# A hand-written order of a linear-attention and feed-forward block, laid out anew behind unchanged loads

## The chip, the cores and the metric

One core of a Trainium2 chip runs the whole program. The metric is the device time of one execution in microseconds (us); every time below is in us unless marked ns. Five engines work beside each other, each through its own queue in order: TensorE (PE; PEld is its weight load), VectorE (DVE), ScalarE (ACT), GpSimd (POOL) and SyncE (SP), which here only issues DMAs.

## The reference

Two blocks in a row on x of 2048 x 512, in bfloat16. Block A is linear attention with 32 heads of 16, block B a feed-forward layer with ReLU of width 1792. Both normalise their input and add their result to it.

```python
qkv = layernorm(x) @ wqkv                    # q, k, v: 32 heads of 16
phi = lambda t: where(t > 0, t + 1, exp(t)) + 1e-6
pq, pk = phi(q), phi(k)
kv = einsum("bhsd,bhse->bhde", pk, v)        # over all 2048 tokens
z = einsum("bhsd->bhd", pk)
o = einsum(pq, kv) / (einsum(pq, z) + 1e-6)
h = x + o @ wo
out = h + maximum(layernorm(h) @ w1, 0) @ w2
```

## The kernel before

The 2048 tokens are 16 tiles of 128 (index t, 0 to 15), four to a chunk (index c, 0 to 3). The program is a list of words in the string ORDER (lines 18 to 53). A word such as K.5.1 calls op_K(5, 1), which issues a few instructions of one engine. The last numbers of a TensorE word name one of the eight banks of the matmul memory, bk; of an ACT or DVE word, how many tiles or banks it takes at once. Each engine runs its own words in the order of the list. Where a word needs what another engine or a DMA makes, or a buffer or bank that another engine still reads, it waits, and everything behind it on its engine waits too. So the list fixes five queues and the use of the banks, and nothing else of the time.

Phase 1, per tile: S and A (lines 237, 238) are the statistics of the norm and their aggregate on VectorE, R (line 257, two activations at 243 and 244) the reciprocal deviation on ScalarE, N (line 260) the normalised tile on VectorE, written to h_nat. It is transposed into lnT either on TensorE and copied out by ScalarE (T, E: lines 284, 290; tiles 0 to 3) or by a transposing DMA (X, line 302; tiles 4 to 15). K (line 306) is the product with the weights of k, four matmuls of 128x512. F is its exponential and U its ReLU on ScalarE (lines 328, 331), M clips the exponential and D adds the two on VectorE (lines 335, 338): the feature map pk. W (line 343) does ReLU and addition in one. G (line 360) adds pk's product with the normalised tile into banks 4 to 7 over all 16 tiles. za and zf (lines 367, 371) add pk up for z on VectorE, z (line 377) finishes it on TensorE, zc and zh copy and mask it (lines 386, 389). Q with qF, qU, qM, qD, qW is the same as K, F, U, M, D, W for the queries, by chunk and by column block.

Phase 2: gA (line 394) copies the sum of G out on ScalarE, kv (line 400) multiplies it by the weights of v, kx masks it, m (line 413) multiplies by wo, mA copies that out. Per chunk, dn (line 454) is the denominator on TensorE, dnl and dnx (lines 464, 470) its logarithm and the exponential of its negative on ScalarE, written to wk_sb, two tiles a word. It is transposed into rd by DMA (dt, line 489) or on TensorE with a copy (rt, rv, re). rd holds one chunk. dm (line 493) multiplies the queries by it, h (line 501) is the product with m, and hD (line 510) adds x.

Phase 3: s, a, n (lines 239, 240, 268) are the second norm; its deviation r (line 258) is used at the end. n is transposed by DMA (x, line 303) or on TensorE (t, e). p (line 517) is the product with w1, pA or pD its ReLU on ScalarE or VectorE (lines 526, 531), f (line 537) the product with w2, fourteen matmuls in two halves, fo (line 547) the scaling and addition on VectorE, fd (line 554) the store. Tile 15 is done in a half and two quarters, a quarter last.

Loads are DMAs of SyncE: lx (x), lk, lq, lv, lo, l1, l2 (weights). Matmuls on zeros (warm, warmf, lines 213 and 218) run until the first tile comes.

```python
for word in ORDER.split():
    name, *idx = word.split(".")
    ops[name](*map(int, idx))
```

Of the kernel before, what the change touches and what calls it, by code (L numbers as in the profile page):

```python
# [38 lines left out]
p.0.10.3 hD.8 dt.15 s.8 a.6 pD.0.6.2 a.4 pA.0.10.2 n.6 f.1.1.0.7 hD.9 n.7 f.1.1.7.7 s.9 dm.3.0.2 dm.3.2.2 h.11.7  # L39
a.5 n.5 h.12.2 h.15.6 h.14.4 fo.1 h.10.5 hD.11 f.0.7.0.7 hD.12 x.6 a.8 h.13.1 a.9 f.3.3.0.7 f.3.3.7.7 x.7 hD.15  # L40
n.4 hD.14 f.0.7.7.7 x.4 f.2.0.0.7 hD.13 fo.3 x.5 p.1.0.6 s.12 s.11 n.8 hD.10 fo.0 p.1.1.7 a.11 fd.0 p.1.5.3 s.10
pD.1.0.2 f.2.0.7.7 a.12 n.12 n.9 s.14 p.1.4.2 n.11 p.1.8.4 fo.2 p.1.3.1 r.4.4 a.10 a.14 p.1.13.7 p.1.2.0
pD.1.4.2 n.10 x.10 x.11 s.13 p.1.7.2 p.1.9.5 p.1.12.6 a.13 pD.1.2.2 s.15 a.15 pD.1.8.2 n.14 pD.1.12.2 p.1.6.1
n.15 x.9 x.8 pA.1.6.2 f.7.0.0.7 p.1.10.4 fd.1 p.1.11.5 pD.1.10.2 fd.3 f.5.2.0.7 p.2.9.7 p.2.11.5 f.7.0.7.7
f.5.2.7.7 fo.7 p.2.8.6 p.2.10.4 p.2.5.1 pD.2.10.2 p.2.4.0 r.8.4 pA.2.8.2 f.4.4.0.7 fo.5 p.2.2.5 fd.2 pA.2.4.2
p.2.3.6 n.13 f.4.4.7.7 p.2.1.3 x.12 p.2.0.2 f.6.0.0.7 x.14 pA.2.2.2 fo.4 x.13 x.15 p.3.3.7 p.3.7.5 p.3.2.6
r.12.4 p.3.9.4 f.6.0.7.7 pA.2.0.2 p.3.11.1 p.3.8.3 p.3.4.2 fd.4 fd.5 fo.6 pA.3.8.2 pD.3.2.2 p.3.10.0 p.3.5.3
p.3.6.4 pA.3.10.2 fd.7 pA.3.6.2 p.2.6.6 pD.3.4.2 p.2.7.7 pD.2.6.2 p.3.13.5 p.3.1.1 fd.6 p.2.12.6 p.3.0.0
# [543 lines left out]
```

## Time and profile before

| what | us |
|---|---|
| median of 3 runs | 170.09 |
| lowest, highest run | 170.05, 170.57 |
| span of the profiled execution, first to last instruction | 168.8 |
| TensorE busy in it | 163.1 |
| VectorE busy | 104.4 |
| ScalarE busy | 65.1 |

The page gives no other time for the profiled execution than its span; the runs' median lies 1.3 above it. A line of the views has a start and a length in us, then engine, source line, operation, what is written and read, shapes and the count of instructions; brackets give idle time of the engine just before and what ended it. The ends of matmuls are modelled: a group of them is through for the next one earlier than its row ends.

### The profile page before, as it was taken

The page shows a single profiled execution, that of the slowest core. Times are in us where ns is not written, and L with a number is a line of the kernel's source. Part 1 is how long each engine was busy: PE and PEld are TensorE (multiplying, and loading weights), DVE is VectorE, ACT ScalarE, POOL GpSimd, SP SyncE. Part 2 cuts the span into 40 slices and gives each one's busy share as a digit, 9 for nine tenths or more (in the row PEclk, how much of TensorE's full clock was granted, in tenths as well). Part 3 has the DMA queues.
Part 4 walks back from the last instruction along what each step waited for, and adds up shares of the span by engine and source line. Part 5 has one row for each costly group of instructions (what it writes and reads, how often), then busy time and mean ns, then how long its engine had stood idle before and what let it go on. Part 6 is the DMA issues. An engine that isn't in the chain of part 4 may idle for free.

```text
span 168.8 us, 2286 instructions
## 1 busy us (share of the span) xinstructions
PE 163.1 (97%) x855; PEld 78.0 (46%) x871; DVE 104.4 (62%) x205; ACT 65.1 (39%) x97; POOL 4.8 (3%) x21
## 2 busy tenths in 40 slices
...
DMA packets 30491, 15.49 MB, mean 92 GB/s; under 512 B 23184, under 2 KB 29328, under 8 KB 30480
## 3 DMA queue, kind: packets, MB, share of 16 engines
...
q8 instruction: 7, 0.11, 0.3%
...
HBM read 7.86 MB, written 2.10 MB: 59 GB/s over the span
## 4 chain that ended last, share of the span: by engine, by line
PE 85%; DVE 7%; DMA 4%; issue 1%; SPq 0%
PE bk L541 29%; PE bk L521 28%; PE bk L505 8%; PE bk L318 8%; PE bk L362 6%; PE bk L310 4%; DVE st L237 3%; DMA x_nat<-in_A_x_dram 2%; DMA lnT<-h_nat 2%; DVE h_nat L262 2%; PE bk L459 1%; DVE eb L335 1%; PE bk L403 1%; PE bk L415 1%; SPq L201 0%
## 5 line engine op out<-in xcount | busy, mean ns | idle before, releaser
L541 PE MATMUL bk<-w_sb,at 128*128 128x512 bf16 (+2 forms) x247 | 50.1, 355 | 0.3
L521 PE MATMUL bk<-lnT,w_sb 128*128 128x512 bf16 x219 | 50.0, 379 | 0.3
L527 ACT ACTIVATE at<-bk 128x1024 bf16<-128x1024 f32 x14 | 14.2, 1023 | 57.4 <-PE bk L521 57.4
L541 PEld LDWEIGHTS <-at 128*128 128x128 bf16 x252 | 23.6, 98 | 25.4 <-ACT at L527 0.3
L549 DVE SCALAR_TENSOR_TENSOR gT<-bk,rstd,h_nat 128x512 bf16<-128x512 f32 (+2 forms) x18 | 12.2, 689 | 35.7 <-PE bk L541 35.6
L521 PEld LDWEIGHTS <-w_sb 128*128 128x128 bf16 x224 | 21.8, 98 | 25.8
L532 DVE TENSOR_SCALAR at<-bk 128x1024 bf16<-128x1024 f32 x14 | 17.1, 1218 | 12.8 <-PE bk L521 12.6
L328 ACT ACTIVATE eb<-bk 128x1024 bf16<-128x1024 f32 (+1 forms) x18 | 16.6, 928 | 6.6 <-PE bk L310 4.8
L310 PE MATMUL bk<-wk_sb,lnT 128*128 128x512 bf16 x63 | 15.3, 380 | 0.4 <-ACT lnT L291 0.3
L505 PE MATMUL bk<-m_sb,pqs 128*128 128x512 bf16 x63 | 15.4, 380 | 0.1
L318 PE MATMUL bk<-lnT,wq_sb 128*128 128x512 bf16 x61 | 15.1, 379 | 0.1
L362 PE MATMUL bk<-at,h_nat 128*128 128x512 bf16 x55 | 13.5, 379 | 0.1
L331 ACT ACTIVATE rb<-bk 128x1024 bf16<-128x1024 f32 (+1 forms) x14 | 12.5, 904 | 0.3 <-PE bk L310 0.3
L511 DVE TENSOR_TENSOR h_nat<-bk,x_nat 128x512 bf16<-128x512 f32 x16 | 10.5, 680 | 2.9 <-PE bk L505 2.9
L237 DVE BATCH_NORM_STATS2 st<-x_nat 128x6 f32<-128x512 bf16 x16 | 10.8, 680 | 2.4 <-DMA x_nat<-in_A_x_dram 2.4
L239 DVE BATCH_NORM_STATS2 st<-h_nat 128x6 f32<-128x512 bf16 x16 | 10.7, 683 | 0.1
L310 PEld LDWEIGHTS <-lnT 128*128 128x128 bf16 x64 | 6.0, 98 | 8.4 <-ACT lnT L291 1.0
L362 PEld LDWEIGHTS <-h_nat 128*128 128x128 bf16 x64 | 6.2, 98 | 7.4 <-issue 0.2
L505 PEld LDWEIGHTS <-pqs 128*128 128x128 bf16 x64 | 5.9, 98 | 7.9 <-DVE pqs L495 1.8
L318 PEld LDWEIGHTS <-wq_sb 128*128 128x128 bf16 x64 | 5.9, 98 | 6.4
L472 ACT ACTIVATE wk_sb<-ld 128x1024 bf16<-128x1024 f32 x8 | 8.1, 1050 | 0.1
L335 DVE TENSOR_SCALAR eb<-eb 128x1024 bf16<-128x1024 bf16 (+1 forms) x18 | 6.8, 383 | 0.9 <-ACT eb L328 0.9
...
## 6 DMA issues: line engine op xcount, KB each, us to landing
...
w_sb<-in_B_w_dram SPq DMA_DIRECT2D x2, 384.0 KB, 3.5
...
```

Source lines behind the costliest of these rows:

```text
L237: op_S = lambda t: nc.vector.bn_stats(out=st[:, t, :], in_=x_nat[:, t, :])
L310: nc.tensor.matmul(bk[:, b, :], lhsT=lnT[c][:, kd, j * P : (j + 1) * P], rhs=wk_sb[:, kd, :], start=(kd == 0), stop=(kd == KD - 1),)
L318: nc.tensor.matmul(bk[:, b, :], lhsT=wq_sb[:, kd, j * P : (j + 1) * P], rhs=lnT[c][:, kd, :], start=(kd == 0), stop=(kd == KD - 1),)
L328: nc.scalar.activation(out=buf(eb, kind, i, n), in_=bank(at_bank[kind, i], n), func=ACT.Exp)
L331: nc.scalar.activation(out=buf(rb, kind, i, n), in_=bank(at_bank[kind, i], n), func=ACT.Relu)
L362: nc.tensor.matmul(bk[:, KD + kd, :], lhsT=ln_nat[:, t, kd * P : (kd + 1) * P], rhs=pk(t)[:, 0, :], start=(t == 0), stop=(t == NT - 1),)
L505: nc.tensor.matmul(bk[:, b, :], lhsT=pqs[:, (c * KD + jb) % NQ, j * P : (j + 1) * P], rhs=m_sb[:, jb, :], start=(jb == 0), stop=(jb == KD ...
L521: nc.tensor.matmul(bk[:, b, cols], lhsT=w1_sb[:, kd, f * P : (f + 1) * P], rhs=lnT[c][:, kd, cols], start=(kd == 0), stop=(kd == KD - 1),)
L527: nc.scalar.activation(out=acts[c % 2][:, f : f + n, :], in_=bank(at_bank["p", c, f], n), func=ACT.Relu)
L532: nc.vector.tensor_scalar(out=acts[c % 2][:, f : f + n, :], in0=bank(at_bank["p", c, f], n), scalar1=0.0, scalar2=None, op0=ALU.max,)
L541: nc.tensor.matmul(bk[:, b, 0 : w * P], lhsT=acts[c % 2][:, f, j * P : (j + 1) * P], rhs=w2_sb[:, f, k * P : (k + w) * P], start=(f == 0), ...
L549: nc.vector.scalar_tensor_tensor(out=o_t[:, t % NO, cols], in0=bk[:, at_bank["f", t, k], 0 : w * P], scalar=rstd2[:, t : t + 1], in1=h_nat ...
```

## The change

Nothing but ORDER changes. The words are the same 547 with the same arguments, apart from the bank numbers of TensorE's words. The loads of x and of the weights of k and q stand in SyncE's queue as before; the twelve X keep their order. In the ramp, the statistics and the normalisation of tile 1 (S.1, A.1, N.1) come ahead of the statistics of tiles 2 and 3, of which tile 3 is first; one warm-up matmul moves from ahead of T.0 to behind T.2; K.1 and K.3 come ahead of T.2. Later, Q.1.1 moves behind kv, qF.1.0 behind both dnx of chunk 0, the weight loads l2.7.3 and l2.0.3 to either side of dt.0 and dt.1, the two other h groups' order and that of dt, p, f, fo and fd change, and two more p groups of chunk 0 stand ahead of the first h of chunk 2. Two lines of ORDER fewer are needed, so that line numbers after it fall by 2.

```diff
 ORDER = """
-const lx.0.1 lx.1.1 warmf.4.3 warm.1.3 S.0 table A.0 R.0.1 S.1 lx.2.2 lk.0.2 warm.1.3 N.0 A.1 S.2 R.1.1 lk.2.2
-lx.4.2 A.2 T.0.7 E.0 warm.1.3 S.3 R.2.1 K.0.1.0.2 lx.6.2 A.3 R.3.1 K.0.1.2.2 N.1 T.1.5 F.0.1 E.1 N.2 N.3 T.3.2
-lx.8.4 E.3 S.4 S.5 A.4 T.2.5 lx.12.4 lq.0.2 A.5 K.1.0.0.2 R.4.2 S.6 M.0.1 N.5 S.7 N.4 X.5 E.2 U.0.1 D.0.1 K.3.7
-K.1.0.2.2 F.3.1 M.3.1 X.4 K.2.3.0.2 U.3.1 A.7 A.6 K.2.3.2.2 U.1.1 R.6.2 F.2.1 F.1.1 G.0 D.3.1 G.3 S.9 U.2.1 N.7
-N.6 S.8 K.5.1 K.4.0 M.2.1 A.8 A.9 R.8.2 U.4.2 M.1.1 X.7 D.2.1 F.4.2 D.1.1 N.9 S.12 X.6 N.8 X.9 G.2 K.7.3 S.13
-A.12 A.13 G.1 R.12.2 K.6.2 K.9.1 M.4.2 S.10 F.6.2 N.12 D.4.2 S.11 A.10 U.6.2 X.8 M.6.2 N.13 G.4 X.12 K.8.0 A.11
-R.10.2 S.14 D.6.2 G.5 G.6 X.13 N.10 N.11 S.15 F.8.2 M.8.2 X.11 A.15 U.8.2 A.14 D.8.2 R.14.2 G.7 za.2 za.4 K.12.0
...
-qU.0.2.2 lo.0.2 z.3.1.14 z.2.1.14 G.15 z.1.1.14 z.0.1.14 qD.0.2.2 zc gA.0.2 gA.2.2 Q.1.0.2 zh dn.0.1 Q.1.1.3
-dnl.0 kv.2.7 lo.2.2 kv.1.7 kv.3.7 dnx.0.2.2 qF.1.0.2 kv.0.7 l2.3.4 dnx.0.0.2 Q.1.2.0 l1.2.2 rt.2.6 kx qM.1.0.2
-Q.1.3.1 qF.1.2.2 m.0.4 m.1.5 rv.2 Q.3.1.7 qW.1.0.2 m.3.6 Q.2.3.2 dt.3 qM.1.2.2 mA.0.2 qW.1.2.2 dt.0 dt.1 m.2.5
-Q.2.1.4 dn.1.0 mA.2.2 dm.0.0.2 Q.2.2.1 dm.0.2.2 dnl.1 dnx.1.2.2 h.3.6 dnx.1.0.2 h.1.5 rt.6.3 hD.3 qF.2.2.2 dt.7
...
-p.0.13.7 p.0.1.6 p.0.8.2 p.0.9.3 dnx.2.0.2 qD.3.0.2 s.4 l2.7.3 p.0.11.4 pA.0.0.2 dt.11 l2.0.3 dt.9 dt.10 r.0.4
-qM.3.2.2 qW.3.2.2 s.6 dt.8 p.0.12.6 s.7 pD.0.12.2 p.0.3.1 p.0.2.0 pA.0.8.2 dn.3.2 p.0.5.7 dnl.3 p.0.4.6 a.7
-dm.2.0.2 pA.0.2.2 dnx.3.0.2 dnx.3.2.2 dm.2.2.2 pD.0.4.2 h.9.0 h.8.5 p.0.6.6 p.0.7.7 dt.13 dt.12 s.5 dt.14
...
-f.15.5.0.14.2.1 fd.13 fd.14 fd.15.0.2 fo.15.2.1 fd.15.2.1
+lx.0.1 lx.1.1 lx.2.2 lk.0.2 lk.2.2 lx.4.2 lx.6.2 lx.8.4 lx.12.4 const warmf.4.5 warm.1.0 S.0 A.0 table R.0.1 S.1 A.1
+N.0 R.1.1 N.1 S.3 A.3 T.0.3 warm.1.1 T.1.6 E.0 R.3.1 S.2 A.2 N.3 K.0.2.0.2 K.0.2.2.2 T.3.3 S.4 S.5 A.4 A.5 E.1 R.2.1
+E.3 U.0.1 F.0.1 R.4.2 N.2 K.1.1.0.2 K.1.1.2.2 K.3.7 T.2.6 E.2 warm.1.3 K.2.2.0.2 K.2.2.2.2 S.7 F.3.1 U.3.1 N.5 M.0.1
+N.4 D.0.1 S.6 M.3.1 A.7 A.6 U.2.1 R.6.2 F.2.1 F.1.1 U.1.1 D.3.1 G.0 G.3 S.9 N.7 S.8 M.1.1 A.9 A.8 N.6 R.8.2 D.1.1
+M.2.1 N.9 D.2.1 lq.0.2 X.5 X.4 X.7 S.13 N.8 S.12 X.6 X.9 X.8 K.5.2 K.4.1 F.4.2 U.4.2 M.4.2 D.4.2 A.12 A.13 R.12.2 G.1
+G.2 K.7.3 K.6.2 F.6.2 U.6.2 G.4 K.9.1 K.8.0 S.10 N.12 N.13 S.11 A.10 M.6.2 A.11 D.6.2 R.10.2 F.8.2 U.8.2 N.11 S.15
...
+W.14.2 zf.12 qF.0.2.2 qU.0.2.2 qM.0.2.2 qD.0.2.2 G.13 G.12 G.14 G.15 z.2.3.14 z.3.3.14 z.1.3.14 z.0.3.14 zc zh gA.0.2
+gA.2.2 Q.1.0.2 dn.0.5 dnl.0 dnx.0.2.2 dnx.0.0.2 l1.0.2 l2.10.4 lo.0.2 lo.2.2 l2.3.4 l1.2.2 dt.3 l2.7.3 dt.0 dt.1
+l2.0.3 kv.1.4 kv.0.4 kv.2.4 kv.3.4 Q.1.1.3 qF.1.0.2 rt.2.7 kx rv.2 m.0.6 Q.1.2.0 Q.1.3.1 m.1.7 Q.2.1.4 m.2.5 qM.1.0.2
+qW.1.0.2 qF.1.2.2 qM.1.2.2 qW.1.2.2 mA.0.2 Q.2.3.2 m.3.6 Q.3.1.7 mA.2.2 dm.0.0.2 dn.1.3 Q.2.2.1 dnl.1 dnx.1.0.2
+dnx.1.2.2 qU.2.2.2 qF.2.2.2 dm.0.2.2 h.1.3 hD.1 s.1 h.0.0 hD.0 rt.6.5 h.3.6 a.1 hD.3 s.0 n.1 a.0 s.3 n.0 qM.2.2.2
...
+dnl.3 pA.0.0.2 p.0.13.5 p.0.6.0 p.0.4.2 p.0.5.3 dt.8 dt.9 dt.10 dt.11 s.5 s.6 hD.7 pD.0.12.2 p.0.7.1 p.0.8.6 p.0.10.4
+p.0.11.5 s.7 pD.0.4.2 dm.2.0.2 dnx.3.2.2 pA.0.8.2 pA.0.10.2 a.7 s.4 a.6 a.4 a.5 n.7 n.6 dm.2.2.2 n.5 pD.0.6.2 p.0.2.3
+h.10.7 h.8.2 p.0.3.4 h.11.1 r.4.4 dnx.3.0.2 pA.0.2.2 dt.14 dt.13 dt.15 dt.12 hD.10 hD.8 s.10 a.10 h.9.0 hD.11 n.10
+s.11 s.8 f.1.5.0.7 f.0.3.0.7 f.0.3.7.7 hD.9 a.11 dm.3.0.2 dm.3.2.2 a.8 fo.0 h.15.0 h.13.1 s.9 hD.15 hD.13 a.9 n.8
+h.14.3 h.12.0 hD.14 n.4 f.2.1.0.7 f.3.6.0.7 f.2.1.7.7 f.1.5.7.7 hD.12 s.12 s.13 s.14 a.14 fo.2 a.13 s.15 n.9 fo.1 x.6
+x.7 x.4 x.10 x.8 x.5 f.3.6.7.7 p.1.8.4 p.1.13.1 p.1.9.5 n.13 n.14 a.12 fo.3 n.11 x.9 fd.3 x.13 x.11 fd.1 p.1.4.6
...
+f.13.2.0.7 f.12.5.7.7 f.14.6.0.7 f.14.6.7.7 f.13.2.7.7 fo.15.2.1 fo.8 fd.15.2.1 fo.11 fd.10 fd.11 fd.8 fd.5 fo.12
+fo.14 fo.13 fd.12 fd.14 fd.13 f.15.3.0.14.0.2 fo.15.0.2 fd.15.0.2 f.15.5.0.14.3.1 fo.15.3.1 fd.15.3.1
 """
```

More of the change, by code (lines that the diff above doesn't have):

```diff
@@ L24 @@
-A.12 A.13 G.1 R.12.2 K.6.2 K.9.1 M.4.2 S.10 F.6.2 N.12 D.4.2 S.11 A.10 U.6.2 X.8 M.6.2 N.13 G.4 X.12 K.8.0 A.11
-R.10.2 S.14 D.6.2 G.5 G.6 X.13 N.10 N.11 S.15 F.8.2 M.8.2 X.11 A.15 U.8.2 A.14 D.8.2 R.14.2 G.7 za.2 za.4 K.12.0
-G.9 K.13.1 N.15 N.14 X.10 lq.2.2 K.11.3 F.12.2 K.10.2 M.12.2 U.12.2 F.10.2 masks X.15 X.14 lv.0.2 lv.2.2 l1.0.2
-U.10.2 za.6 D.12.2 M.10.2 G.8 za.8 D.10.2 Q.0.1.1 Q.0.0.0 qF.0.0.2 qU.0.0.2 za.10 G.12 K.14.2 K.15.3 Q.0.2.0
-za.12 Q.0.3.1 G.13 F.14.2 G.11 qF.0.2.2 l2.10.4 qM.0.0.2 M.14.2 W.14.2 zf.12 G.10 qD.0.0.2 qM.0.2.2 G.14
@@ L29 @@
-qU.0.2.2 lo.0.2 z.3.1.14 z.2.1.14 G.15 z.1.1.14 z.0.1.14 qD.0.2.2 zc gA.0.2 gA.2.2 Q.1.0.2 zh dn.0.1 Q.1.1.3
-dnl.0 kv.2.7 lo.2.2 kv.1.7 kv.3.7 dnx.0.2.2 qF.1.0.2 kv.0.7 l2.3.4 dnx.0.0.2 Q.1.2.0 l1.2.2 rt.2.6 kx qM.1.0.2
-Q.1.3.1 qF.1.2.2 m.0.4 m.1.5 rv.2 Q.3.1.7 qW.1.0.2 m.3.6 Q.2.3.2 dt.3 qM.1.2.2 mA.0.2 qW.1.2.2 dt.0 dt.1 m.2.5
-Q.2.1.4 dn.1.0 mA.2.2 dm.0.0.2 Q.2.2.1 dm.0.2.2 dnl.1 dnx.1.2.2 h.3.6 dnx.1.0.2 h.1.5 rt.6.3 hD.3 qF.2.2.2 dt.7
-s.3 re.6 h.0.0 dt.4 qU.2.2.2 hD.1 dt.5 a.3 hD.0 s.1 s.0 a.1 qM.2.2.2 a.0 Q.3.0.6 Q.2.0.3 n.3 h.2.5 n.0 dm.1.0.2
@@ L34 @@
-Q.3.3.1 x.3 dm.1.2.2 qF.3.0.2 hD.2 n.1 s.2 Q.3.2.0 qU.2.0.2 qF.2.0.2 h.5.2 h.6.3 a.2 qU.3.0.2 qM.2.0.2 h.4.7 n.2
-qF.3.2.2 x.0 qD.2.0.2 t.2.5 qD.2.2.2 hD.4 x.1 hD.6 h.7.4 dn.2.6 hD.5 hD.7 e.2 dnl.2 qM.3.0.2 p.0.0.5 dnx.2.2.2
-p.0.13.7 p.0.1.6 p.0.8.2 p.0.9.3 dnx.2.0.2 qD.3.0.2 s.4 l2.7.3 p.0.11.4 pA.0.0.2 dt.11 l2.0.3 dt.9 dt.10 r.0.4
-qM.3.2.2 qW.3.2.2 s.6 dt.8 p.0.12.6 s.7 pD.0.12.2 p.0.3.1 p.0.2.0 pA.0.8.2 dn.3.2 p.0.5.7 dnl.3 p.0.4.6 a.7
-dm.2.0.2 pA.0.2.2 dnx.3.0.2 dnx.3.2.2 dm.2.2.2 pD.0.4.2 h.9.0 h.8.5 p.0.6.6 p.0.7.7 dt.13 dt.12 s.5 dt.14
@@ L39 @@
[L39 to L48, printed above, removed]
```

16 lines of the change are left out of this document (13 added, 3 removed).

## The prediction

> **What bounds the kernel now.** I read the page first, then the chain of waits, then TensorE's own timeline.
>
> ```profile
> PE 163.1 (97%) x855; PEld 78.0 (46%) x871; DVE 104.4 (62%) x205; ACT 65.1 (39%) x97; POOL 4.8 (3%) x21
> ```
>
> TensorE is busy 97% of the span. The chain in order of time says where it does not set the end:
>
> ```profile
> 5.60 0.71 DVE st L237
> ...
> 17.65 3.40 DMA lnT<-h_nat
> ...
> 21.10 1.04 PE bk L310 x4
> ...
> 166.18 0.35 DVE gT L549
> ```
>
> Up to 17.65 us the chain runs on VectorE, then through one transposing DMA (X.8, 3.40), and from 21.10 to 166.18 it is TensorE. A busy row can still hide waiting, so the rate is needed:
>
> ```profile
> 9.43 2.75 PE L310 MATMUL bk<-wk_sb,lnT 128*128 128x512 bf16 x12
> ...
> 13.85 1.93 PE L310 MATMUL bk<-wk_sb,lnT 128*128 128x512 bf16 x8
> ...
> 19.94 1.03 PE L362 MATMUL bk<-at,h_nat 128*128 128x512 bf16 x4
> ...
> 41.37 0.54 PE L459 MATMUL bk<-zhd,pqT 128*128 128x8 bf16 x16
> ...
> 49.54 0.81 PE L318 MATMUL bk<-lnT,wq_sb 128*128 128x512 bf16 x3
> 50.25 2.07 PE L505 MATMUL bk<-m_sb,pqs 128*128 128x512 bf16 x8
> ...
> 69.81 1.89 PE L521 MATMUL bk<-lnT,w_sb 128*128 128x512 bf16 x8
> 71.62 2.07 PE L505 MATMUL bk<-m_sb,pqs 128*128 128x512 bf16 x8
> ```
>
> Twelve matmuls take 2.75 and four 1.03, so one costs (2.75 - 1.03) / 8 = 0.215 and a group of four 0.86. G.4, at 19.94, is through at 20.80 and K.8 starts at 21.10: **0.30 lost**. Eight back to back take 1.89. The eight of h.3 and h.1 (line 505) take 2.07, and start 0.06 after 49.54 + 3 x 0.215: **0.24 lost**. The same sum for the first two groups of h.8 to h.11, at 71.62, gives 0.18 + 0.09 = **0.27 lost**. VectorE has the reason of these two: dm waits for the transposes dt.
>
> ```profile
> 49.50 1.29 DVE L495 TENSOR_TENSOR pqs<-pqT,rd 128x1024 bf16<-128x1024 bf16 x2 [1.02 <-DMA rd<-wk_sb]
> ...
> 70.88 1.29 DVE L495 TENSOR_TENSOR pqs<-pqT,rd 128x1024 bf16<-128x1024 bf16 x2 [1.61 <-DMA rd<-wk_sb]
> ```
>
> I count 0.81 us of waiting between 13.85 and 72. The change issues the same operations, word for word apart from banks, so the work stays and only TensorE's waits can move. I add those up, place by place.
>
> **The change part by part: the ramp.**
>
> ```profile
> 4.63 0.41 DVE L262 TENSOR_SCALAR h_nat<-x_nat,mv,rstd 128x512 bf16<-128x512 bf16 x1
> ...
> 5.60 0.70 DVE L237 BATCH_NORM_STATS2 st<-x_nat 128x6 f32<-128x512 bf16 x1 [0.47 <-DMA x_nat<-in_A_x_dram]
> ...
> 7.23 1.09 DVE L262 TENSOR_SCALAR h_nat<-x_nat,mv,rstd 128x512 bf16<-128x512 bf16 x3
> ...
> 8.24 1.28 DVE L237 BATCH_NORM_STATS2 st<-x_nat 128x6 f32<-128x512 bf16 x2
> ...
> 13.33 0.72 DVE L262 TENSOR_SCALAR h_nat<-x_nat,mv,rstd 128x512 bf16<-128x512 bf16 x2
> ```
> ```profile
> 5.17 0.29 ACT L243 ACTIVATE rstd<-mv,eps 128x1 f32<-128x1 f32 x1 [0.57 <-DVE mv L238]
> 5.49 0.20 ACT L244 ACTIVATE rstd<-rstd 128x1 f32<-128x1 f32 x1
> ...
> 6.34 0.60 ACT L291 ACTIVATE lnT<-bk 128x512 bf16<-128x512 bf16 x1 [0.64 <-PE bk L281]
> ```
>
> Before, VectorE idles 0.47 until tiles 2 and 3 land, and N.1 comes after both their statistics (three N in 1.09, so 0.34 apart). After, A.1 directly follows S.1, the pair R.1 (5.17 to 5.69, so 0.52) ends near 5.4, and N.1 runs in that idle time. The next statistics start at 5.73 instead of 5.60. VectorE gains 0.34 - 0.13 = 0.21.
>
> What is late next is N.5. It needs R.4, and ScalarE now has E.1, R.2, E.3, U.0 and F.0 ahead of that pair. Two statistics with aggregates take 5.60 to 7.23, so N.3 runs from 5.73 + 1.63 = 7.4 to 7.8, T.3 takes about 0.4 and E.3 starts at 8.2; with 0.6 for it, 0.5 for each of U.0 and F.0 (they overlap a little) and 0.52 for R.4, that ends at 10.3. VectorE is ready for N.5 at 10.05: N.3 is off at 7.7, then three statistics at 0.6 (two in 1.28), two aggregates at 0.1 and N.2. So it loses 0.25 and the gain is gone; N.7 (13.33 now), behind the same VectorE instructions as before, comes about 0.1 later.
>
> TensorE transposes tile 0 one warm-up matmul earlier (0.43, below), but then waits about 0.65 for E.2 ahead of K.2, and G.3 waits for D.3, which VectorE delivers no earlier than now. K.5 starts near 13.85 as before, and from there to the end of K.9 every input and bank is ready first: 0.
>
> **X.8.** SyncE's queue holds X.5, X.4, X.7, X.6, X.9, X.8 in the old order. X.7 waits for N.7, the others for the issue ahead of them, so X.8 starts at 17.65 to 17.85. Its landing is bounded by:
>
> ```profile
> L302 SPq DMA_TRANSPOSE lnT<-h_nat x12: 1188/1208/1282, 10.9 to 28.9; - x12
> ...
> DMA to landing us min/median/max: 2.4/2.5/4.1
> ```
>
> At 2.5 it lands near 20.3, ahead of K.8's place at 20.8, and the 0.30 goes. At 3.40, as here, K.8 still waits 0.3 to 0.45; at 4.1 about 1. I take 2.5, the median. The page has a candidate for the late ones:
>
> ```profile
> q8 instruction: 7, 0.11, 0.3%
> ```
>
> These seven packets are 16 KB each and share the DMA engines; whether one hits X.8 depends on the moment, which the views do not give. The Trainium skill (Runtime: NRT & Kernel Launch, Instruction fetch mechanics) says that a sequencer fetches its own code blocks over its own DMA queue and that crossing a block is mostly hidden. By that rule the late landing has another cause and stays, which is rival 2; a landing of 3.40 beside a median of 2.5 does not look hidden, but no row ties the two together.
>
> **dn.0 and kv.** Before, Q.1.0 and Q.1.1 cover the way from G.15 over z, zc, zh and gA; now Q.1.1 stands behind kv.
>
> ```profile
> 40.07 1.94 ACT L395 ACTIVATE gT<-bk 128x1024 bf16<-128x1024 f32 x2 [2.15 <-PE bk L362]
> ...
> 42.35 1.06 ACT L472 ACTIVATE wk_sb<-ld 128x1024 bf16<-128x1024 f32 x1
> 43.31 1.01 ACT L328 ACTIVATE eb<-bk 128x1024 bf16<-128x1024 f32 x1
> 44.21 1.05 ACT L472 ACTIVATE wk_sb<-ld 128x1024 bf16<-128x1024 f32 x1
> ```
> ```profile
> 28.41 0.43 DVE L335 TENSOR_SCALAR eb<-eb 128x1024 bf16<-128x1024 bf16 x1 [0.53 <-ACT eb L328]
> ...
> 40.95 0.29 DVE L390 TENSOR_TENSOR zhd<-mask_h,z_sb 128x128 bf16<-128x128 bf16 x1
> ...
> 45.15 1.22 DVE L343 SCALAR_TENSOR_TENSOR pqT<-bk,eb 128x1024 bf16<-128x1024 f32 x1
> ```
>
> dn.0 starts at 41.37 now, right behind Q.1.0 and 0.13 after zh. TensorE, 0.30 ahead, would be ready at 41.07. VectorE's queue is full from 14 to 41: the 0.53 that it idles at 28.41 goes, but it starts 0.1 later, waits about 0.2 for F.10 and has more dependent pairs side by side (M.4-D.4, S.14-A.14, za.4-za.6, M.10-D.10). An instruction behind an independent one starts about 0.08 before that ends, and a dependent one after it, so each pair costs about 0.1. zh ends between 40.7 and 41.3; I take 41.24, as now, nearest to the row. dn.0 then waits **+0.30**. kv, whose gA now ends 0.4 earlier than at 42.01, adds nothing behind that; if zh were early, kv would still wait for gA until 41.5.
>
> qF.1.0 (43.31 now) moves behind both dnx, to 44.2 to 45.25; qM.1.0 and qW.1.0 (0.43 + 0.1 + 1.22) take it to 47.0. Q.2.3 needs their bank. Its place is 47.0 too: four groups (0.86, 0.215, 0.86 and dn.1's 0.38) ahead of Q.2.2, which starts one matmul before 49.54. With 0.06 for the release I take **+0.10** (0 to 0.2).
>
> **l2.7.3 ahead of dt.0 and dt.1.**
>
> ```profile
> 43.43 4.86 SPq L491 DMA_TRANSPOSE rd<-wk_sb x3
> 60.09 0.57 SPq L204 DMA_DIRECT2D w_sb<-in_B_w_dram  x1
> ```
> ```profile
> w_sb<-in_B_w_dram SPq DMA_DIRECT2D x2, 384.0 KB, 3.5
> ```
> ```profile
> L491 SPq DMA_TRANSPOSE rd<-wk_sb x14: 1188/1210/1759, 43.4 to 76.1; - x14
> ...
> DMA to landing us min/median/max: 2.4/2.5/3.6
> ```
>
> dt.3 issues at 43.43 for 1.2, and dt.0 waits now for dnx.0.0 (44.21 + 1.05). After, dnx.0.0 ends at 44.3, but l2.7.3 takes SyncE from 44.65 for 0.57, so dt.0 and dt.1 start at 45.3 and 46.5 as now, with 384 KB queued ahead. dt.1 lands between 46.5 + 2.4 = 48.9 and 46.5 + 3.6 = 50.1; I take 49.45, where dm starts now. dm.0 then ends at 50.1 and 50.8, against h.1's place at 50.3 and that of its third matmul at 50.7: **+0.10** instead of 0.24. The weights ahead start 1.3 earlier, since X.15 and X.14 do; TensorE waits for none of them: 0.
>
> **From h to the end.** n.1 and n.0 move ahead of hD.2 and n.2, which now come close to h.4 and t.2, and e.2 and qD.2 close to dn.2; the margins are under 0.1 each: **+0.10** for the three (0 to 0.3). Before h.10 stand two more p groups than before h.9 now, so h.10 comes at 71.5 + 1.7 = 73.3 with its third matmul at 73.7. dt.8 to dt.11 are no longer interrupted by l2.0.3 and land near 70; dm.2 is done at 73.2, 4 us of VectorE work after p.0.5. The 0.27 goes. In the p and f groups every bank is free before its next use; the nearest input is x.5. From h.14 to its landing: 1.3 to n.4, three transposes at 1.21 to 1.28, and 2.5, together 7.6; to p.1.8 TensorE has h.12 and five f halves of 7 x 0.215, together 8.4. The last quarter of tile 15, its addition (0.35 at 166.18) and store are the same: 0.
>
> **Sum**: -0.30 - 0.24 - 0.27 + 0.30 + 0.10 + 0.10 + 0.10 = **-0.21 us**. The profiled span of 168.8 becomes 168.6. The runs' median, 170.09, lies 1.3 above that span; with the same 1.3 the forecast is **169.9**.
>
> **The rivals.**
> 1. Slower: dt.1 lands late behind the 384 KB. At 50.1, dm.0 ends at 50.8 and 51.5; h.1 starts 0.5 late and its third matmul waits 0.2 more: 0.7 over the forecast with what follows, **170.6**. It decides from a landing after 49.5. For it: dm already waits 1.02 here, and some dt took 3.6; against: the loads ahead are 1.3 earlier.
> 2. X.8 lands late again. K.8 waits 0.4, K.10 and F.10 come later by that, M.10 stops VectorE and zh with it: 0.2 over, **170.1**.
> 3. Faster: VectorE keeps the 0.53. dn.0 waits 0, kv 0.15 for gA, Q.2.3 and h.1 nothing: 0.35 under, and 0.1 more if the three small waits stay away, **169.5**.
> 4. Slower: TensorE stays at its half rate longer.
>
> ```profile
> 4.82 1.06 PE L215 MATMUL bk<-m_sb 128*128 128x512 bf16 x2
> ...
> 6.99 1.05 PE L310 MATMUL bk<-wk_sb,lnT 128*128 128x512 bf16 x4 [0.26 <-ACT lnT L291]
> ```
>
> Two warm-up matmuls take 1.06, where eight at the full rate take 1.89: 0.43 apart, half rate. K.0's four in 1.05 are at the full rate. After, K.0 starts at 6.6, ahead of that. If the rate rises 3 us later, twelve matmuls cost 0.215 more each; of these 2.6 most falls into the waits for E.2 and D.3, and about 0.9 reaches N.5 and N.7: **170.8**. The Trainium skill (TensorE: Matmul & The Clock Gate, Part 1: The HAM clock gate) states such a rule: the clock rises after some 3.4 us of work in a free-running window, so the point varies from run to run. The rows agree with one rise before 7.0; one execution cannot show the spread.
>
> **How the numbers follow.** Forecast 0.45 (169.7 to 170.2), rival 1 0.20, rival 2 0.10, rival 3 0.20, rival 4 0.05. The bounds of the small waits reach 0.2 beyond rivals 3 and 1, so the range is 169.3 to 170.8. About 0.3% (0.5 us) is what a measurement of this kernel can tell from no change. Faster by more: most of rival 3, 0.22 with a tail of the forecast. Slower by more: rivals 1 and 4 and the same tail, 0.28. Within: 0.50.
>
> **What would show it.** Right: K.8 directly behind K.9 near 20.8, a gap of 0.3 on TensorE before dn.0, h.10 without a gap, nothing later. Wrong: a p or f group that waits for a DMA or an activation, N.7 before 13.2, dm.0 starting after 49.8.

## The result, and the profile after

| | before | after |
|---|---|---|
| median | 170.18 (20 runs) | 170.71 (20 runs) |
| lowest to highest | 169.84 to 170.81 | 169.95 to 171.81 |
| ratio to before, 95% interval | 1 | 1.0033 (1.0017 to 1.0048) |
| profiled execution: time, span | not given, 168.8 | 171.31, 169.6 |

The change costs 0.5 us, where 0.2 less was forecast. The spread grows with it: 1.9 between the lowest and the highest run instead of 1.0. A run's time lies 1.7 above its span, so both profiled executions lie above the median of their kernel: that of before, at about 170.5, by 0.3 and that of after by 0.6.

The page of after shows the same work, TensorE busy as before:

```profile
PE 163.1 (96%) x855; PEld 77.9 (46%) x871; DVE 104.7 (62%) x205; ACT 65.1 (38%) x97; POOL 4.8 (3%) x21
```

So the 0.8 between the spans is waiting of TensorE. Its timeline in after, at the places that the prediction went through (start, length, engine, line, operation; line numbers are 2 less than before):

```profile
14.06 1.89 PE L308 MATMUL bk<-wk_sb,lnT 128*128 128x512 bf16 x8
...
19.24 1.03 PE L360 MATMUL bk<-at,h_nat 128*128 128x512 bf16 x4
20.11 1.89 PE L308 MATMUL bk<-wk_sb,lnT 128*128 128x512 bf16 x8
21.83 2.75 PE L360 MATMUL bk<-at,h_nat 128*128 128x512 bf16 x12
24.42 2.83 PE L308 MATMUL bk<-wk_sb,lnT 128*128 128x512 bf16 x11
27.51 1.04 PE L308 MATMUL bk<-wk_sb,lnT 128*128 128x512 bf16 x4 [0.26 <-DMA lnT<-h_nat]
28.39 1.03 PE L360 MATMUL bk<-at,h_nat 128*128 128x512 bf16 x4
...
40.88 1.02 PE L316 MATMUL bk<-lnT,wq_sb 128*128 128x512 bf16 x4
41.74 0.54 PE L457 MATMUL bk<-zhd,pqT 128*128 128x8 bf16 x16
...
49.74 1.02 PE L316 MATMUL bk<-lnT,wq_sb 128*128 128x512 bf16 x3
51.27 2.07 PE L503 MATMUL bk<-m_sb,pqs 128*128 128x512 bf16 x8 [0.50 <-DVE pqs L493]
```
```profile
74.28 1.89 PE L503 MATMUL bk<-m_sb,pqs 128*128 128x512 bf16 x8
```

K.9 and K.8 are eight matmuls in 1.89 without a gap: the 0.30 at K.8 is gone. dn.0 starts 0.86 after Q.1.0, four matmuls of 0.215: no gap. h.10 and h.8 take 1.89: the 0.27 is gone too. But from 24.42 to 28.39 stand the sixteen matmuls of K.12, K.13, K.11 and K.10, 3.45 of work in 3.97: **0.52 lost**, at a place for which the prediction had no term. And Q.2.2, at 49.74, four matmuls of which one has no row, is through at 50.60; h.1 starts 0.67 later and takes 2.07 instead of 1.89 together with h.0, which stands behind it in after: **0.85 lost**, where 0.10 was forecast.

The views lack the rows of a few matmuls. The weight loads show the first of these two places most clearly, since none of them is missing; the first fence is after, the second before:

```profile
24.21 1.61 PEld L308 LDWEIGHTS <-lnT 128*128 128x128 bf16 x8
26.21 0.55 PEld L308 LDWEIGHTS <-lnT 128*128 128x128 bf16 x4 [0.40 <-DMA lnT<-h_nat]
27.51 0.55 PEld L308 LDWEIGHTS <-lnT 128*128 128x128 bf16 x4 [0.75 <-DMA lnT<-h_nat]
```
```profile
24.35 0.75 PEld L310 LDWEIGHTS <-lnT 128*128 128x128 bf16 x4
25.21 0.74 PEld L362 LDWEIGHTS <-h_nat 128*128 128x128 bf16 x4
26.07 2.47 PEld L310 LDWEIGHTS <-lnT 128*128 128x128 bf16 x12
```

In after, K.11 at 26.21 and K.10 at 27.51 wait for X.11 and X.10. In before, G.9 stands behind K.12 and the next three K follow in 2.47 without a wait.

For the second place, VectorE and SyncE in after:

```profile
50.53 1.29 DVE L493 TENSOR_TENSOR pqs<-pqT,rd 128x1024 bf16<-128x1024 bf16 x2 [1.46 <-DMA rd<-wk_sb]
```
```profile
43.80 2.10 SPq L489 DMA_TRANSPOSE rd<-wk_sb  x1
45.94 0.58 SPq L202 DMA_DIRECT2D w_sb<-in_B_w_dram  x1
46.62 2.50 SPq L489 DMA_TRANSPOSE rd<-wk_sb  x2
```

dt.3's issue takes 2.10 instead of 1.2, l2.7.3 follows, and dt.1 lands at 50.45 (49.45 was forecast).

Why were X.12, X.13 and dt.3 slow? The DMA view of after between 20 and 24 us (40 slices of 0.1; busy tenths, then GB/s), and under it that of e10, an experiment below in which TensorE's code is fetched 1.2 earlier:

```profile
DMA  0000020000000062999999960000000001016999
GB/s 0 0 0 0 0 82 0 0 0 0 0 0 0 0 164 51 192 197 212 197 202 138 34 0 3 5 8 10 10 10 8 10 10 13 0 20 102 202 200 210
...
q8 instruction: 1, 0.02, 1.6%
q14 instruction: 1, 0.01, 0.7%
...
lnT<-h_nat SPq DMA_TRANSPOSE x3, 3.2
```
```profile
DMA  0006000010000003899997210000038999983000
GB/s 0 0 0 164 0 0 0 0 82 0 0 0 0 0 0 51 179 218 225 205 215 169 46 4 0 0 0 0 0 49 174 223 218 207 215 179 45 3 0 0
...
q8 instruction: 1, 0.02, 1.5%
q14 instruction: 1, 0.01, 0.5%
...
lnT<-h_nat SPq DMA_TRANSPOSE x3, 2.4
```

A transpose moves its packets in one burst of 0.8, after its issue. In after, the packet on q8 (16 KB of code, at 21.48; 164 GB/s in the slice before the burst) starts with the burst of X.12, and when the burst is over a trickle of 3 to 13 GB/s goes on for 1.0: a few packets are late. X.12 lands 3.8 after its issue began and X.13's issue takes 1.95. In e10 the q8 packet comes at 20.30, the bursts follow without a trickle, and both land 2.4 after. dt.3 in after shows a third case: the q8 packet, at 44.31, comes 0.51 behind the start of its issue and is not over when its burst begins at 45.0; the issue itself takes 2.10, and dt.3 lands 3.2 after. Which DMA engine carries the late packets the views do not tell.

### The profile page after: what moved, and what is told of

It reads as the page before. It is cut to its first block, busy times and chain, and to the rows that moved or that the text cites. A ratio compares the mean times of both kernels' runs of the same rounds, so it can differ in the third digit from the quotient of the medians.

```text
span 169.6 us, 2285 instructions
## 1 busy us (share of the span) xinstructions
PE 163.1 (96%) x855; PEld 77.9 (46%) x871; DVE 104.7 (62%) x205; ACT 65.1 (38%) x97; POOL 4.8 (3%) x21
## 4 chain that ended last, share of the span: by engine, by line
PE 79%; DVE 11%; DMA 5%; ACT 2%; issue 1%; SPq 0%; DVEq 0%
PE bk L519 28%; PE bk L539 28%; PE bk L503 8%; PE bk L316 6%; DVE st L235 5%; PE bk L360 4%; DVE h_nat L260 2%; PE bk L308 2%; DMA rd<-wk_sb 2%; DMA x_nat<-in_A_x_dram 2%; DMA lnT<-h_nat 1%; DVE eb L333 1%; ACT eb L326 1%; DVE mv L236 1%; PE bk L457 1%
## 5 line engine op out<-in xcount | busy, mean ns | idle before, releaser
L519 PE MATMUL bk<-lnT,w_sb 128*128 128x512 bf16 x220 | 49.8, 379 | 0.2
L539 PE MATMUL bk<-w_sb,at 128*128 128x512 bf16 (+2 forms) x247 | 49.6, 355 | 0.3
L241 ACT ACTIVATE rstd<-mv,eps 128x2 f32<-128x2 f32 (+2 forms) x14 | 4.1, 293 | 13.3 <-DVE mv L238 8.0
```

The costliest lines, as they stand in the source:

```text
L519: nc.tensor.matmul(bk[:, b, cols], lhsT=w1_sb[:, kd, f * P : (f + 1) * P], rhs=lnT[c][:, kd, cols], start=(kd == 0), stop=(kd == KD - 1),)
L539: nc.tensor.matmul(bk[:, b, 0 : w * P], lhsT=acts[c % 2][:, f, j * P : (j + 1) * P], rhs=w2_sb[:, f, k * P : (k + w) * P], start=(f == 0), ...
```

## The experiments

Every kernel but e11 and e13, which repeat after and before, changes only ORDER. To place the losses I subtract from the start of each weight load the matmul work ahead of it (0.216 for 512 columns, 0.056 for 128, 0.024 for the short ones of dn and z); where that lag rises beyond the rise of an execution without a wait and does not fall back, TensorE waited. The table holds these waits, and as the ramp the lag at K.4 less the start of S.0, that is the time from the first statistics to K.4 without the matmul work between; "later" is h.9 in before and p.1.8 in e5.

| run | median, ratio to before | ramp | K.8 | K.12 to K.10 | dn.0 | first h | later |
|---|---|---|---|---|---|---|---|
| before | 170.18 | 4.69 | 0.30 | 0 | 0 | 0.25 | 0.26 |
| e13, before again | one run, 169.52 | 4.24 | 0.29 | 0 | 0 | 0 | 0 |
| after | 170.71, 1.0033 | 4.55 | 0 | 0.52 | 0 | 0.85 | 0 |
| e11, after again | 170.69, 1.0046 | 4.55 | 0 | 0.78 | 0 | 0.29 | 0 |
| e1, weights back | 170.80, 1.0034 | 4.84 | 0 | 0.41 | 0 | 0 | 0 |
| e14, e15, e1 again | one run each, 170.71, 170.68 | 4.56, 4.58 | 0 | 0.75, 1.05 | 0 | 0 | 0 |
| e4, before, weights ahead | 171.01, 1.0057 | 4.79 | 0.33 | 0 | 0 | 1.32 | 0 |
| e5, before, then after | 170.85, 1.0044 | 4.90 | 0.33 | 0 | 0 | 0.62 | 0.22 |
| e6, after, then before | 170.47, 1.0021 | 4.62 | 0 | 0.59 | 0 | 0 | 0 |
| e7, weights back, early N.12 | 170.49, 1.0016 | 4.54 | 0.46 | 0 | 0.11 | 0 | 0 |
| e8, fetch earlier | 170.48, 1.0012 | 4.54 | 0 | 0 | 0.11 | 0.87 | 0 |
| e9, order of x | 170.97, 1.0059 | 4.75 | 0 | 0.82 | 0 | 0.20 | 0 |
| e12, weights back, order of x | 170.90, 1.0043 | 4.60 | 0 | 0.53 | 0 | 0 | 0 |
| e10, e12 and fetch earlier | 170.09, 0.9996 | 4.55 | 0 | 0 | 0.12 | 0.24 | 0 |

**Which half: e4, e5, e6.** e4 is before with

```diff
-qW.1.2.2 dt.0 dt.1 m.2.5
+qW.1.2.2 l2.7.3 dt.0 dt.1 l2.0.3 m.2.5
```

and both loads taken from their later places; e5 and e6 are cut at Q.1.0, with the order of one kernel up to there and of the other behind.

> Before, with l2.7.3 put ahead of dt.0 and l2.0.3 behind dt.1, as in the change, and nothing else. Theory A (these loads delay dt.1): dt.1 lands 0.6 to 0.9 later than before (near 50.2), h.3 and h.1 lose 0.7 to 1.0 instead of 0.24; h.9's 0.27 goes, since l2.0.3 no longer stands between dt.11 and dt.9; time 170.4 to 170.7 against 170.2. Theory B (only the code fetch beside dt.3 does it): h.1 loses at most 0.4, time 170.0 to 170.2.

> Cut at Q.1.0: the order of before up to there, the order of after behind it (with l2.7.3 and l2.0.3 around dt.0 and dt.1). Theory A (the loss is in the two loads): TensorE reaches dn.0 as in before (41.4), h.1 waits 0.7 to 1.2, time 170.7 to 171.0 against 170.2. Theory B (the code fetch decides, wherever it meets transposes): h.1 waits only in executions where the fetch near 44 meets dt.3, 0 to 1.0, median 170.2 to 170.6, spread wider than that of before. Theory C (the loss is ahead of Q.1.0, in X.10 to X.13): 170.0 to 170.2.

> Cut at Q.1.0 the other way: the order of after up to there, the order of before behind it. Theory A: the loss behind Q.1.0 is gone, time 170.0 to 170.3. Theory C (X.12 is issued 1.2 later than in before and K.12 to K.10 stand 0.9 to 1.2 earlier, so the fetch beside X.12 and X.13 makes K.12 to K.10 wait 0.3 to 1.5): 170.6 to 171.0, with the spread of after, and K.11 or K.10 waiting in the profile.

e4 measured 1.0057 (1.0037 to 1.0078), e5 1.0044 (1.0025 to 1.0062), e6 1.0021 (1.0007 to 1.0035). Both halves lose, by the medians: the rear with the weight loads ahead 0.6 to 0.8, the front 0.24. In e4 the rows are

```profile
51.58 2.07 PE L505 MATMUL bk<-m_sb,pqs 128*128 128x512 bf16 x8 [0.97 <-DVE pqs L495]
```
```profile
44.92 0.58 SPq L204 DMA_DIRECT2D w_sb<-in_B_w_dram  x1
45.60 3.25 SPq L491 DMA_TRANSPOSE rd<-wk_sb  x2
```

Two transposes that take 2.5 take 3.25; the q8 fetch comes at 45.38, beside them. The front of after in e6 has the wait at K.12 to K.10 and not the one at K.8. In e5 kv loses 0.18 besides, for which the table has no column: its sixteen matmuls take 1.23 instead of 1.05, since ScalarE ends the second half of gA at 42.23 only. With the rear of after, dt.0 lands 3.15 to 3.61 after its issue where l2.7.3 stands ahead of it (after, e2, e5, e8, e9, e11), and 2.4 after where the loads stand behind x.3 (e1, e7, e10, e12, e14, e15).

**The weight loads alone: e1, and e14 and e15, the same kernel.**

```diff
-l1.2.2 dt.3 l2.7.3 dt.0 dt.1 l2.0.3 kv.1.4
+l1.2.2 dt.3 dt.0 dt.1 kv.1.4
-x.0 x.1 x.3 e.2
+x.0 x.1 x.3 l2.7.3 l2.0.3 e.2
```

> After, with the two weight loads l2.7.3 and l2.0.3 (384 KB each) taken from around dt.0 and dt.1 and put behind x.3. Theory A (the 384 KB ahead of dt.0 and dt.1 delay h.1): dt.0 starts 0.67 earlier and both fly without the load beside them, dt.1 lands by 49.6 instead of 50.45, h.1's wait falls from 0.84 to 0.2 or less, and the time from 170.7 to about 170.1. Theory B (dt.3's issue of 2.10 instead of 1.2, beside the fetch of TensorE's code on queue q8, delays h.1): dt.3 still takes 2.1, dt.1 lands at 49.8 or later, h.1 still waits 0.3 to 0.4, time about 170.3. Neither (the difference between the kernels lies elsewhere): 170.6 to 170.8.

> e1 again: its runs reach from 170.0 to 171.9, and its profile (170.4) came from the lower end. Theory C (the fetch near 21.4 beside X.12 and X.13 makes K.12 to K.10 wait by an amount that varies): an execution of 170.8 or more shows the excess over 0.5 at K.12 to K.10 and nowhere else, about 0.4 for 170.8 and 1.0 for 171.4. Theory E (the excess lies in the ramp): K.4 starts later than 14.9 by that much.

> e1 a third time, for the same question and with the same expectations as e14: any excess over 170.4 at K.12 to K.10 (theory C) or ahead of K.4 (theory E).

dt.1 lands at 48.7 to 49.0 and h.1 never waits, as theory A had it; but the median, 1.0034 (1.0014 to 1.0055), is that of after. e14 and e15 show what remains: their ramps are not late, and theory C holds, with 0.75 and 1.05 at K.12 to K.10. Why the runs as a whole gain nothing stays open, for the three profiles of this kernel wait 0.41 to 1.05 in all and the two of after 1.37 and 1.07. In e15 every one of the four waits:

```profile
24.30 0.55 PEld L308 LDWEIGHTS <-lnT 128*128 128x128 bf16 x4 [0.61 <-DMA lnT<-h_nat]
25.05 0.66 PEld L308 LDWEIGHTS <-lnT 128*128 128x128 bf16 x4 [0.20 <-DMA lnT<-h_nat]
26.35 0.55 PEld L308 LDWEIGHTS <-lnT 128*128 128x128 bf16 x4 [0.64 <-DMA lnT<-h_nat]
27.64 0.55 PEld L308 LDWEIGHTS <-lnT 128*128 128x128 bf16 x4 [0.75 <-DMA lnT<-h_nat]
```

**The same kernels again: e11 and e13.**

> After, unchanged, on this chip beside the others. 0.2 to 0.45% above before. Its profile tells whether the waits of the first profile (0.5 at K.11 and K.10, 0.84 at h.1) come back at the same places: theory B (code fetches meeting transposes, whose moment varies by some tenths) expects the same places with other sizes: 0 to 0.7 at K.12 to K.10, 0.2 to 0.9 at h.1, 0 to 0.5 at p.1.8; theory A expects 0.7 to 0.9 at h.1 each time.

> Before, unchanged, for a second execution: its first profile came from one of its slower executions (span 168.8, where most have 168.3 to 168.5). Theory B (code fetches of varying moment): ramp and K.8 as in the first (K.8 waits 0.3), but h.3 or h.9 without their waits, span 168.2 to 168.5. Otherwise (the waits are set by the order alone): K.8 0.30, h.3 0.24, h.9 0.27 again, and the ramp alone varies.

e11 measured 1.0046 (1.0029 to 1.0064); e13 ran once. The wait at K.12 to K.10 is there in every execution of this front with its fetch in place (0.41 to 1.05 in eight profiles); that at h.1 varies, 0.85 and 0.29 here, as theory B expects: in e11 the fetch came at 43.07, ahead of dt.3, whose issue took 1.2. e13 loses neither 0.25 at h.3 nor 0.26 at h.9: two of the three waits that the change was credited with removing belonged to that one execution. Its ramp is shorter as well:

```profile
4.80 0.60 PE L215 MATMUL bk<-m_sb 128*128 128x512 bf16 x2
...
6.31 1.05 PE L310 MATMUL bk<-wk_sb,lnT 128*128 128x512 bf16 x4 [0.47 <-ACT lnT L291]
```

These two warm-up matmuls took 1.06 in the first profile, and K.0 started at 6.99. So TensorE's rate rose before 4.8 here and between 6.1 and 7.0 there, where the warm-up matmul at 6.10 still takes 0.63, and K.0 starts 0.68 earlier. The ramp of after takes 4.54 to 4.62 in all but e1 and e9, with T.0 at the half rate (after, e11) as with T.0 at the full one (e14, e15). In e1 and e9 (4.84, 4.75) the first tile comes early, S.0 at 3.09 and 3.04, and T.0 and T.1 both still run at the half rate.

**The code fetch: e3, e8, e12 against e10, e18.** e3 replaces all warm-up matmuls by 48 small ones; e8 only

```diff
-warmf.4.5 warm.1.0 S.0
+warmf.4.5 warms.9.0 S.0
```

(warms: nine matmuls of 64 columns). e12 is e1 with the order x.10 x.4 x.5 x.8, e10 is e12 with the edit of e8, and e18 is before with the same edit of its first single warm-up matmul (warm.1.3 becomes warms.9.3).

> After, with the warm-up matmuls replaced by 48 small ones (64 columns): TensorE's program has 89 more rows ahead of the first K, so each of its code fetches (16 KB on q8) comes some 7 us earlier: at about 14.5 and 37 instead of 21.5 and 44.3. Theory B (the fetches hold up transposes that SyncE issues at that moment): X.13's issue takes 1.2 instead of 1.95, X.11 lands at 25.4 and X.10 at 26.7, K.11 and K.10 wait for nothing; dt.3's issue takes 1.2 instead of 2.10 and h.1 waits 0.3 or less; time about 169.9. Theory A (the order of the transposes and loads alone makes them late): the two long issues stay, 170.7. If the small matmuls warm TensorE less, the K groups before 9 us show it as matmuls of 0.43, and some tenths are lost there.

> After with one warm-up matmul of 512 columns replaced by nine of 64: 16 more rows in TensorE's program, so its code fetches come some 1.3 earlier (near 20.2 and 43.0). Theory B: the second fetch is over before dt.3 starts at 43.8, dt.3's issue takes 1.2 instead of 2.1, dt.1 lands near 49.6, and h.1 waits 0.2 or less instead of 0.84; the first one meets X.8 and X.12 instead of X.12 and X.13. Time 170.1 to 170.4. Theory A (the loads alone): h.1 still waits 0.6 or more, 170.7.

> After with the two weight loads behind x.3 (e1) and x.10 x.4 x.5 x.8. Theory D (what e1 saved at h.1 was lost again at p.1.8 in half of its executions): 0.3 to 0.5 below after, about level with before. If p.1.8 is not the place, as e1: level with after, 0.3% above before.

> After with three mends: the two weight loads behind x.3, nine small warm-up matmuls for one long one (the code fetch 1.3 earlier), and x.10 x.4 x.5 x.8. All theories together: no wait at K.12 to K.10, h.1 waits 0.2 or less, p.1.8 never waits; against before the waits of 0.30 (K.8), 0.24 (h.3) and 0.27 (h.9) are gone: 169.5 to 169.8, some 0.5 below before. If the forecast's dn.0 term holds (zh at 41.2 whatever TensorE does), dn.0 waits 0.3 of that: 169.8 to 170.1.

> Before with one of its warm-up matmuls of 512 columns (of three) replaced, three in all by nine of 64, so that its code fetches come about 0.9 earlier; a control for e8, e10, e16 and e17. Theory C: before has room at K.12 to K.10 (X.13 lands 0.8 to 1.3 ahead of K.13), so the shift gains nothing there: 170.0 to 170.4, or some tenths more if the clock rises later for the smaller matmuls. If the small matmuls themselves are what gained in e8 and e10: 169.6 to 169.9.

e3 loses 4.0, 1.0239 (1.0223 to 1.0255): the small matmuls end at 3.35, TensorE idles until 5.31, and its rate stays at one half for K.0:

```profile
6.61 1.89 PE L308 MATMUL bk<-wk_sb,lnT 128*128 128x512 bf16 x4
```

That hides what the fetch does to the time. But the first fetch, 89 rows of TensorE's program earlier, comes at 14.70 and meets X.7 and not X.13: X.7's issue takes 1.82, X.13's 1.22. The stall moved with the fetch, and the fetch with TensorE's rows: in all 20 profiles it comes when TensorE has begun 87 to 93 weight loads. The second fetch did not move as expected: 44.02 in e3, where 37 was expected. The DMA engines are all but full, mainly with weights, until 42.75 there, and until 41.25 to 42 in after, e8, e11 and e16; whether this fetch waits behind those loads no run shows. In e8 the fetch is at 19.86, ahead of X.12's burst, and the sixteen matmuls run through:

```profile
24.06 3.62 PE L308 MATMUL bk<-wk_sb,lnT 128*128 128x512 bf16 x16
```

Its second fetch, at 43.55, still met dt.3, which theory B had not expected (dt.3 itself came 0.8 earlier), and h.1 lost 0.87; 1.0012 (0.9997 to 1.0026). e12 and e10, on the same chip, differ by that edit alone: 1.0043 (1.0027 to 1.0059) and 0.9996 (0.9983 to 1.0009), **0.8 us**. e10 is level with before and no better, against the 0.5 below that was expected: its ramp and waits are 4.91 together, those of before 5.50 in the first profile but 4.53 in e13. The 0.8 is one of medians: the profiled executions of e12 and e10, 170.36 and 170.37, do not differ, since that of e12 is its second shortest of eleven and that of e10, which waits 0.17 less, got its first tile 0.24 later. The control e18 gains nothing from small matmuls, 1.0017 (1.0002 to 1.0032).

**Room instead of another moment: e2, e7.** e2 puts G.9 between K.13 and K.11, as before had it behind K.12, and D.8 ahead of za.2. e7 is e1 with

```diff
-M.4.2 D.4.2 A.12 A.13 R.12.2 G.1
+M.4.2 A.12 A.13 R.12.2 D.4.2 G.1
-K.8.0 S.10 N.12 N.13 S.11 A.10
+K.8.0 N.12 N.13 S.10 S.11 A.10
```

> After, with G.9 put between K.13 and K.11 (and D.8, which it needs, ahead of za.2 on VectorE). Theory A (X.11 and X.10 land later than the place that the change gave K.11 and K.10): K.11 and K.10 come 0.86 later in the order and wait for nothing, 0.5 us goes, and unless zh is late the time falls to about 170.3. Theory B (VectorE's queue up to zh sets dn.0, and the 0.5 only stood ahead of that): the waits for X.11 and X.10 go too, but dn.0 waits 0.3 to 0.5 for zh at 41.6, and the time stays at 170.6 to 170.8.

> After with the two weight loads behind x.3 (as in e1), and on VectorE A.12 and A.13 between M.4 and D.4, N.12 and N.13 ahead of S.10: X.12 starts near 19.65 instead of 20.35. Theory C: X.12 lands by 23.5 and X.13, X.11, X.10 0.5 to 0.7 earlier than in e1, K.12 to K.10 wait 0 to 0.2, and what e1 left goes: 170.0 to 170.3, less what dn.0 then waits for zh (0.2 to 0.3). Otherwise (VectorE sets the pace up to zh): 170.6 to 170.8, with dn.0 waiting 0.4.

e7, 1.0016 (1.0000 to 1.0032), is 0.3 under e1: X.12 starts at 19.38 and lands at 21.80, ahead of the fetch, and K.12 to K.10 wait for nothing; but X.8 now lands 3.36 after its issue, with the 8 KB fetch of q14 at 19.68, and K.8 waits 0.46. e2 measured 1.0059 (1.0042 to 1.0076), worse than both theories. K.11 and K.10 do not wait, but K.12 does, for X.12 (landed 24.51), X.10 comes at 25.37 with lq.2.2 behind it in SyncE's queue, and Q.0.0 waits for the weights. In the waits of its weight loads (total, times, longest):

```profile
PEld L316 <- DMA wq_sb<-in_A_wqkv_dram: 0.8, 1, 0.8
```

With D.8 ahead of za.2, zh ends at 42.14 and dn.0 waits 0.32 for it (it starts at 42.20 instead of 41.88), as theory B said.

**The second transposes: e9.** x.10 x.4 x.5 x.8 instead of x.4 x.10 x.8 x.5.

> After, with the second transposes queued x.10 x.4 x.5 x.8 instead of x.4 x.10 x.8 x.5: x.5, the last that p.1.8 needs, lands near 91.0 instead of 93.5, 2.9 ahead of p.1.8 instead of 0.4. Theory D (in some executions a code fetch near 86 to 89 holds these transposes up and p.1.8 waits 0.3 to 0.8): the median falls by 0.1 to 0.4 against after, and the slowest executions (171.3 to 171.8) by more. Otherwise: as after, 0.3% above before, same spread.

x.5 lands at 90.41, 3.0 ahead of p.1.8, and the time does not fall: 1.0059 (1.0038 to 1.0079). Theory D is wrong as an explanation of the loss, though e5 shows one such wait (p.1.8 starts at 94.16 instead of 93.94, 0.22 lost).

**Towards a better kernel: e16, e17.** e16 is e6 with the edit of e8 and l2.0.3 behind dt.8; e17 is e16 up to e.2 with the order of after from there.

> The order of after up to Q.1.0 with the code fetch moved 1.3 earlier (nine small warm-up matmuls for one long one, as in e8), the order of before behind it, with l2.0.3 put behind dt.8. By theories B and C together no wait is left at K.8, K.12 to K.10 and h.9, and at most 0.25 at h.3: span 168.0, time 169.5 to 169.8, 0.3 to 0.6 below before. If the gain ahead of Q.1.0 is eaten by a wait of dn.0 for zh: 170.0 to 170.2.

> Three pieces: the order of after up to Q.1.0 with the code fetch 1.3 earlier (as e16), the order of before from there to e.2 (dt.0 and dt.1 ahead of the two weight loads, which now stand behind e.2), the order of after from there to the end. By theories B and C no wait is left at K.8, at K.12 to K.10 (0 to 0.2), h.3 or h.10, and the last stores are those of after, away from the fetch that e16 moved onto fd.8: 169.5 to 169.8, 0.3 to 0.6 below before. If it is only the ramp's clock that sets before's median (early rise in half of its executions): level with before, 170.0 to 170.2.

e16 measured 1.0018 (1.0002 to 1.0034). Its waits are 0.10 at K.10 and none behind, and it lost 0.6 against e6 at the end, where its fetch at 161.0 met the store fd.8 and VectorE waited for that buffer:

```profile
163.23 1.91 DVE L547 SCALAR_TENSOR_TENSOR gT<-bk,rstd,h_nat 128x512 bf16<-128x512 f32 x3 [2.37 <-DMA out_dram<-gT]
```

e17, 1.0052 (1.0035 to 1.0069), missed. At its second seam p.0.1 waits for ScalarE's dnl.2,

```profile
62.33 1.89 PE L519 MATMUL bk<-lnT,w_sb 128*128 128x512 bf16 x8 [0.65 <-ACT ld L463]
```

and its first fetch fell 0.3 later than in e16, at 20.66, which brought 0.45 back at K.12 to K.10. No version beats before by more than its interval.

## Why the prediction was wrong, point by point

- **K.8, -0.30: right.** X.8 lands 2.42 after its issue and K.8 does not wait. The prediction could not say what made it late before. It is the 8 KB fetch of q14: in before, e4, e5, e7, e13 and e18 it comes 1.8 to 2.0 after X.8's issue begins, and X.8 lands 3.3 to 3.5 after; in all the others it comes when X.8 is down, and X.8 lands 2.4 after. The change won here because it moved that fetch by 1.0 (19.53 to 20.56). In all 20 profiles this fetch comes 0.20 to 0.50 behind the start of X.12's issue, so what moved it is that X.12 starts 1.2 later: the 0.30 won at K.8 and the loss at K.12 to K.10 have one source, and e7, which starts X.12 at 19.38 again, gets the wait at K.8 back.
- **"From there to the end of K.9 every input and bank is ready first: 0": this held, but stopped too early, and that is the step that failed.** Behind K.9 the sum had no term up to dn.0. There the change moves G.9 from behind K.12 to behind K.10, so that K.13, K.11 and K.10 come 0.86 earlier, and N.12 ends at 20.32 instead of 19.13, so that X.12 starts 1.2 later. In before X.13 landed at 25.25, 4.1 after its issue began, and nobody waited, because K.13 stood at 26.07: a late landing with 0.8 of cover. The page's maximum of 4.1, with which I bounded X.8, belonged to X.13. Measured: +0.41 to +1.05.
- **h.1, +0.10: the mechanism of rival 1, with a size that varies.** dt.1 lands at 49.80 to 50.45 in after, e9 and e11 (rival 1 decided from 49.5), and h.1 waits 0.20 to 0.85. dm.0 at 50.53 and 49.88 are past the 49.8 that the prediction named as the sign of error. The loads ahead, 0.67 of SyncE's time, use up the margin, and the fetch beside dt.3 decides how much shows. With the loads behind x.3 h.1 waits 0, or 0.24 where the fetch still meets dt.3 (e10).
- **dn.0, +0.30: too large.** It is 0 in after, where the loss ahead of it hides what there is (zh ends at 41.63, and TensorE reaches dn.0 at 41.74), and 0.11 to 0.12 in e7, e8 and e10, where that loss is gone. Which part of the 0.30 was too large the runs do not separate. Q.2.3: 0.05 instead of 0.10.
- **h.10, -0.27, and the small waits: right for this pair of executions.** h.4, t.2 and dn.2 wait for nothing. But e13 has no wait at h.9 or h.3: 0.5 of the 0.81 that could go is not there in that execution of before, at 169.52 below its median.
- **The ramp, ±0: about right on average, for another reason.** After needs 4.55 mostly, before 4.24 to 4.90 by the moment at which TensorE's rate rises. Rival 4 looked for this in after, with whose front it is worth 0.2 to 0.3 (e1, e9); with that of before it is worth up to 0.66. The Trainium skill (TensorE: Matmul & The Clock Gate, Part 1: The HAM clock gate) says that the moment depends on where in a free-running window the first matmul falls and varies by 0.5 either way. The two executions of before agree that it varies, but lie at least 1.3 apart (the full rate before 4.8, the half rate still at 6.1), more than the page gives; here the measurement decides.
- **The sum for the two profiles**: ramp 0.15 (the first tile came 0.29 later, the way from it was 0.14 shorter), K.8 -0.30, K.12 to K.10 +0.52, h +0.60, h.9 -0.26, together +0.71 of the 0.75 between the spans. For the two repeats, e11 less e13: +0.33, -0.29, +0.78, +0.29, together 1.11 of 1.14. The medians differ by 0.5. That after's median lies near the 170.6 of rival 1 is in part luck: rival 1 had the whole loss at h.1, and 0.52 and 0.78 of it lie at K.12 to K.10.

The prediction weighed the rule of the Trainium skill (Runtime: NRT & Kernel Launch, Instruction fetch mechanics) that a block crossing is mostly hidden. For the engine that fetches this holds: TensorE shows no gap at 21.48 in after. For the DMAs that the fetch meets it does not: 1.0 of trickle behind X.12's burst, 2.10 instead of 1.2 for dt.3, 3.4 instead of 2.4 for X.8. Here the measurement decides.

What stays open: why the same 16 KB hold a transpose up by 0.2 at most when they come at the start of its issue, by 0.8 in the middle of it and by up to 1.9 when they come with its burst; why e1 is no faster than after; and how often before takes the quick ramp of e13, and so how its median divides between ramp and waits, for which two profiles are not enough.
